# A planned order for the first attention pairs, one index table, two expert halves in a row, and unread matrix products in the tail

## The chip, the cores and the metric

The kernel runs on one core of one Trainium2 chip. The metric is the device time of one execution in microseconds; lower is better. The core's engines work side by side and wait for each other by semaphores: PE (TensorE, matrix products into PSUM), DVE (VectorE), ACT (ScalarE), POOL (GpSimd, which here issues all loads) and SP (SyncE, which issues the stores).

## The reference

Attention over 4 batches of 8 heads, 768 positions of 64 numbers, causal. In some heads ("streaming") a position sees only the first 4 keys and the last 64. Its output, as 3072 rows of 512, goes through a soft mixture of 8 experts with 4 slots each:

```python
scores = np.where(mask, q @ k.T / 8, -1e9)          # mask: causal, or sinks and window
a = softmax(scores);  x = (a @ v)                    # -> x: [3072, 512]
logits = x @ phi                                     # [3072, 32 slots]
d = exp(logits) / column sums;   slot_input = d.T @ x
for e in range(8):
    slot_out[e] = relu(slot_input[e] @ w1[e]) @ w2[e]    # 512 -> 1024 -> 512
out = (exp(logits) / row sums) @ slot_out
```

## The kernel before

**Pairs and quads.** Two heads make a pair (`n`, 16 of them), two pairs a quad (`Q`, 8), four pairs a batch (`b`). For a quad, `load` (L203) brings q, k and v, converting f32 to bf16 on the way; each of the three has two buffers (`raws`), so the load for quad Q + 2 is issued when quad Q has been read (`after_turn`, L560). The first quad is loaded in halves. POOL issues these loads in order, with the expert weights between them (`weights`, L537). The buffers and the mask table lie in the space of the last four w2 matrices, which are therefore loaded last (L571 to L575, L624).

**Steps of a pair.** In the plan's names: `T` turns half a quad of q, k or v with PE transposes (L221), and `e` copies the result from PSUM to SBUF on DVE or ACT (L233). `Tb`/`eb` turn v back into blocks (L244, L252). `Q` makes a unit of 448 score columns for both heads (L268), `x` its exp on ACT (L280), `M` multiplies the four kinds of block by the mask (L286), `V` makes a masked copy of v (L260). `P` is the product with v (L304), `N` divides by the row sum (L315), `X`/`eX` transpose the output (L326, L336). Per batch, `La`, `Lb` and `el` give the logits and their exp, `G`, `D`, `R` the sums over them. `H` builds one head's mask from the tables `delta` and `stream` (`head_mask`, L525, two DVE operations of 256 columns).

**Order.** Nothing is scheduled at run time: class `Plan` (L42) holds the operations of PE, ACT and DVE with costs, dependences, earliest times (`at`) and ranks, and walks through them, always taking the one that can start first. The engines get their work in that order and follow it strictly. PSUM has two slots for scores (`sc`) and two for transposes (`tr`); an operation that takes a slot waits until its former contents are read.

**Before the plan** (L473 to L553): the constants are set, ten products of zeros keep PE busy, q and k of the first half quad are turned, the tables are made on DVE from three index patterns written by POOL, and the masks of heads 0 to 3 are built. The masks of heads 4 to 7 are `H` steps of the plan.

**After the plan** (L624 on): the last batch's dispatch (`slp`), its sums, the slot inputs `siT`; for each half of the experts (`e4`) the product with w1 (`hp`, L665, 32 products of 512 columns), relu on ACT and DVE (`hs`), transposes (`tph`) and their copy `hT`; the product with w2 (`second`, L682) in four calls; the output rows, stored as they come (L704).

Of the kernel before, what the change touches and what calls it, by code (L numbers as in the profile page):

```python
# [38 lines left out]
SWITCH = 0.115  # L39


class Plan:  # L42
# [22 lines left out]
    def build(self):  # L65
        NP, add = self.NP, self.add
        for n in range(NP):
            Q, b, n4 = n // 2, n // 4, n % 4
            for u in range(6):
                if Q:  # L70
                    d = [f"e{t}{Q}.{h}" for t in "qk" for h in range(2)]
                else:
                    d = [f"e{t}0.1" for t in "qk"] if n else []
                add(f"Q{n}.{u}", "PE", 0.19, 0.27, d, n + u / 6, "Q", mode="H", slot=("sc", f"x{n}.{u}"))
                d = [f"Q{n}.{u}"] + ([f"P{n - 2}.1.B"] if u == 0 and n > 1 else [])
                add(f"x{n}.{u}", "ACT", 0.814, 0.95, d, n + u / 6, "x")
            if 2 <= n < 4:
                for a in range(2):
                    add(f"H{n}.{a}", "DVE", 0.8, 0.9, [], n - 1.0, "H")
            hm = [f"H{n}.0", f"H{n}.1"] if 2 <= n < 4 else []  # L80
# [16 lines left out]
        for i, t in enumerate("vqk"):  # L97
            if t == "v":
                self.turn(t, 0, 0, [], 0.0, cost=0.5)
            self.turn(t, 0, 1, [], {"v": 1.0, "q": 0.3, "k": 0.6}[t], cost=0.5)  # L100
        for a in range(2):
            self.turn("b", 0, a, [f"ev0.{a}"], a + 0.5)
        for Q in range(1, NP // 2):
            n = 2 * Q - 1
            for i, (t, h) in enumerate((("q", 0), ("k", 0), ("q", 1), ("k", 1))):
                d = [f"Q{2 * Q - 3}.5"] if Q > 1 else []
                self.turn(t, Q, h, d, n + i / 4, at=(4.0 if t == "q" else 6.0) if Q == 1 else 0.0)
            for h in range(2):
                d = [f"Tb{Q - 1}.1"]
                self.turn("v", Q, h, d, n + 1 + h / 4, at=8.0 if Q == 1 else 0.0)  # L110
            for a in range(2):
                d = [f"P{2 * Q - 3}.1.B", f"V{2 * Q - 3}"] if Q > 1 else []
                self.turn("b", Q, a, [f"ev{Q}.0", f"ev{Q}.1"] + d, n + 1.5 + a / 4)
        for b in range(NP // 4):
# [4 lines left out]
            if b < NP // 4 - 1:  # L119
# [5 lines left out]
                add(f"eR{b}", "DVE", 0.15, 0.25, [f"R{b}"], n + 2.1, "eD")  # L125

    def order(self):
# [44 lines left out]
RANK = {"D": -0.22, "V": 1.15, "x": 2.77, "M": -1.62, "eX": 0.07, "eD": 0.79, "M5": -0.31, "eT": -0.45,  # L172
        "X": 0.66, "P": 0.44, "G": 0.12, "el": -0.31, "L": -0.76, "H": -0.26, "N": -0.18, "eG": 0.8,
        "T": -0.79}
EVAC = {"k1": "ACT"}
# [3 lines left out]
class Attn:  # L179
# [57 lines left out]

    def copy(self, eng, o, i):
        if eng == "ACT":
            self.nc.scalar.copy(o, i)  # L240
        else:
            self.nc.vector.tensor_copy(o, i)  # L242
# [37 lines left out]
    def exp(self, n, u):  # L280
        if u == 0:
            self.pT[n] = self.ptp.tile([128, 2, NPT], BF16, tag="pT", name="pT")
        self.nc.scalar.activation(self.pT[n][:, :, u * UNIT:(u + 1) * UNIT], self.sc.pop((n, u))[:, :, :UNIT],  # L283
                                  ACT.Exp, scale=self.scale)
# [113 lines left out]
def kernel(  # L398
# [75 lines left out]
    nc.sync.dma_start(ri, bass.AP(tensor=ir32, offset=0, ap=[[0, P], [1, 2 * H]]))  # L474
    at.load("q", 0, 0)
    at.load("k", 0, 0)
    with tc.tile_pool(name="setup", bufs=1) as setup:
        iti = setup.tile([P, P], I32, name="iti")
        nc.gpsimd.iota(iti, pattern=[[1, P]], base=0, channel_multiplier=-1)
        at.load("v", 0, 0)  # L480
        at.load("q", 0, 1)
        at.load("k", 0, 1)
        nc.gpsimd.iota(tk[:, 0:1], pattern=[[0, 1]], base=0, channel_multiplier=1)
        tq = setup.tile([P, 256], I32, name="tq")
        nc.gpsimd.iota(tq, pattern=[[128, 2], [1, 16], [16, 8]], base=0, channel_multiplier=0)
        at.load("v", 0, 1)

        zw = msk[:, H - 1, :]
        nc.vector.memset(zw, 0.0)
        zp = at.scp.tile([P, 2, 512], F32, tag="sc", name="zp")  # L490

        def zeros(c):
            for i in range(c):
                nc.tensor.matmul(zp[:, i % 2, :], zw[:, :128], zw, start=True, stop=True)  # L494

        zeros(10)
        nc.vector.memset(quarter, 0.25)
        nc.scalar.activation(colpart[:, 0:1], quarter, ACT.Exp)
        for vb in vbs:
            nc.vector.memset(vb[:, :, :, :, 64:], 1.0)  # L500
        nc.vector.tensor_single_scalar(ident, iti, 0.0, op=ALU.is_equal)
        at.turn("q", 0, 0)
        at.turned("q", 0, 0, "DVE")
        at.turn("k", 0, 0)
        at.turned("k", 0, 0, "ACT")
        zeros(2)

        nc.vector.tensor_single_scalar(tk[:, 1:2], tk[:, 0:1], 7, op=ALU.bitwise_and)
        nc.vector.tensor_single_scalar(tk[:, 2:3], tk[:, 0:1], 3, op=ALU.logical_shift_right)
        nc.vector.tensor_single_scalar(tk[:, 3:4], tk[:, 1:2], 4, op=ALU.logical_shift_left)  # L510
        nc.vector.tensor_tensor(tkf[:, 0:1], tk[:, 2:3], tk[:, 3:4], op=ALU.add)
        nc.vector.tensor_single_scalar(tkf[:, 1:2], tkf[:, 0:1], float(n_sink), op=ALU.is_lt)
        nc.vector.tensor_tensor(tkf[:, 2:3], tkf[:, 0:1], tk[:, 0:1], op=ALU.subtract)
        nc.vector.tensor_scalar(perm, iti, tkf[:, 2:3], None, op0=ALU.is_equal)
        causal = setup.tile([P, 256], BF16, name="causal")
        nc.vector.tensor_scalar(causal, tq, tkf[:, 0:1], 0.0, op0=ALU.subtract, op1=ALU.is_ge)
        nc.vector.tensor_scalar(delta, tq, tkf[:, 0:1], float(window), op0=ALU.subtract, op1=ALU.is_ge)
        nc.vector.tensor_sub(stream, causal, delta)
# [4 lines left out]
    nc.vector.tensor_copy(fmask[:, :, 0], r0)  # L523

# [4 lines left out]

    for t in "qkv":  # L530
        at.load(t, 1)
    for h in (0, 2, 1, 3):
        head_mask(h)
# [8 lines left out]
    phf = at.small.tile([P, 4, ES], F32, tag="phf", bufs=1, name="phf")  # L542
    for hp in range(2):
        for qh in range(2):
            nc.sync.dma_start(phf[64 * hp:64 * hp + 64, 2 * qh:2 * qh + 2, :],
                              moe_phi.rearrange("(qh hp a d) s -> qh hp d a s", qh=2, hp=2, a=2)[qh, hp])
    weights(1)
    nc.gpsimd.tensor_copy(phi, phf)
# [5 lines left out]


# [22 lines left out]
    for name in plan.order():  # L578
# [26 lines left out]
        elif op == "R":  # L605
            at.row_sums(int(arg))
        elif op == "T":
# [3 lines left out]
            else:  # L611
                at.turn(t, Q, h)
                turns[t, Q] = turns.get((t, Q), 0) + 1
                if turns[t, Q] == (1 if Q == 0 and t != "v" else 2):
                    after_turn(t, Q)
        elif arg[0] in "qkvb":
# [20 lines left out]
    at.exp_slots_out(bl)  # L637
    for e4 in range(2):
# [15 lines left out]
    nc.vector.tensor_copy(siT, sip)  # L654
    sctx.close()
# [3 lines left out]
    hTs = []  # L659
    for e4 in range(2):  # L660
# [11 lines left out]
        hv = hs.rearrange("p c f -> p (c f)").rearrange("p (fi fo) -> p fo fi", fo=8)  # L672
        tp = at.trp.tile([P, 8, P], BF16, tag="tr", name="tph")
        for fo in range(8):
            nc.tensor.transpose(tp[:, fo, :], hv[:, fo, :], ident)
# [103 lines left out]
```

## Time and profile before

| | us |
|---|---|
| median of 3 runs | 162.59 (161.79, 167.25, 162.59) |
| the profiled execution | 162.0 |
| its span, first to last instruction | 160.3 |
| busy in the span: PE / DVE / ACT / POOL | 127.5 / 117.1 / 107.4 / 30.6 |
| first exp, last exp (start) | 11.24, about 113.7 |
| first store issued | 140.58 |

Times of single steps are microseconds from the span's start. In a line of the timeline stand the start, the time from first start to last end, the engine, the line, the operation, output and input, how many, and in brackets how long the engine was idle before and what ended that. Matmuls are pipelined, so the shown times of neighbours overlap; the pitch, from one start to the next, is what a queue of them takes. PEclk is the granted clock of PE, 1.00 or 10 tenths being full. DMA moved 26.22 MB of loads by the software queue; its busy share was 0.9 or more in nearly every slice from 4 us to 128 us, and 6.29 MB of output went out after 140.6 us.

The chain of work that ended last is 50% PE, 25% DVE and 16% ACT.

### The profile page before, as it was taken

How to read it: one execution, taken by the hardware profiler on the slowest of the kernel's cores; microseconds unless marked ns; L12 is line 12 of the kernel's file. 1: busy time of each engine (PE TensorE's matmuls, PEld its weight loads, DVE VectorE, ACT ScalarE, POOL GpSimd, SP SyncE). 2: the span in 40 equal slices, each digit the busy share in tenths (PEclk: the TensorE clock that was granted, in tenths of full speed). 3: DMA queues.
4: the chain of work that ended last, by engine and by line, in shares of the span. 5: the costliest groups of instructions: out<-in, count | busy, mean ns of one | idle time of the engine just before them, and what ended most of it. 6: DMA issues, size and time to landing. Idle time of an engine off the chain costs nothing.

```text
span 160.3 us, 5605 instructions
## 1 busy us (share of the span) xinstructions
PE 127.5 (80%) x2506; PEld 87.9 (55%) x2508; DVE 117.1 (73%) x256; ACT 107.4 (67%) x141; POOL 30.6 (19%) x58
## 2 busy tenths in 40 slices
PE   6765999999999998999999998998744866886200
PEld 2344666777777675676777675675532235752000
DVE  1499877999999988999989999978845031267400
ACT  3030779999899988999989998989603014087600
POOL 6941432041050033036200013000510000000000
PEclk9955558999999999999999999999996599999955
DMA  2999999999999999999999999999999960069996
GB/s 35 187 168 213 225 199 230 198 224 208 206 224 203 214 229 197 225 210 204 222 212 220 217 221 211 217 215 217 219 194 196 201 85 0 4 203 342 367 404 255
DMA packets 16087, 32.93 MB, mean 205 GB/s; under 512 B 1728, under 2 KB 8896, under 8 KB 14272
## 3 DMA queue, kind: packets, MB, share of 16 engines
q0 software_dynamic: 11216, 26.22, 86.4%
q1 hardware_dynamic: 4848, 6.37, 11.5%
q8 instruction: 19, 0.31, 0.7%
q14 instruction: 4, 0.03, 0.1%
HBM read 52.50 MB, written 6.29 MB: 367 GB/s over the span
## 4 chain that ended last, share of the span: by engine, by line
PE 50%; DVE 25%; ACT 16%; issue 3%
ACT pT L283 11%; PE sc L276 11%; PE pv L311 9%; DVE pT L302 5%; DVE xb L323 5%; PE tpv L228 3%; PE hp L665 3%; PE tpk L228 3%; PE tpx L332 3%; PE tpq L228 3%; PE zp L494 3%; PE sp L687 3%; DVE w L527 2%; PE tpb L248 2%; ACT ot L731 2%
## 5 line engine op out<-in xcount | busy, mean ns | idle before, releaser
L283 ACT ACTIVATE pT<-sc 128x896 bf16<-128x896 f32 x96 | 81.6, 922 | 9.6 <-PE sc L276 7.8
L276 PE MATMUL sc<-qT,kT 64*128 64x128 bf16 (+4 forms) x352 | 34.2, 281 | 1.1 <-ACT pT L283 0.6
L302 DVE TENSOR_TENSOR pT<-pT,w 128x1024 bf16<-128x1024 bf16 (+1 forms) x64 | 32.1, 519 | 3.3 <-ACT pT L283 2.7
L311 PEld LDWEIGHTS <-pT 128*128 128x128 bf16 x672 | 25.1, 97 | 10.1 <-issue 7.8
L311 PE MATMUL pv<-vb,pT 128*128 128x65 bf16 x352 | 28.7, 193 | 1.2 <-DVE xb L323 1.1
L228 PEld LDWEIGHTS <-w 96*64 96x64 bf16 (+1 forms) x864 | 22.7, 121 | 9.4 <-issue 5.9
L311 PE MATMUL pv<-vf,pT 128*128 128x65 bf16 x320 | 24.4, 194 | 0.3 <-issue 0.3
L276 PEld LDWEIGHTS <-kT 64*128 64x128 bf16 x352 | 12.3, 96 | 8.4 <-issue 1.4
L323 DVE TENSOR_TENSOR xb<-pv,rs 128x768 bf16<-128x768 f32 x16 | 15.3, 957 | 0.6
L240 ACT COPY kT<-tpk 128x768 bf16<-128x768 bf16 x9 | 7.2, 799 | 9.6 <-PE tpk L228 9.6
L208 POOL DMA_DIRECT2D w<-in_q_dram x7 | 4.6, 657 | 35.8 <-PE sc L276 31.9
L263 DVE TENSOR_TENSOR vf<-vb,fmask 128x528 bf16<-128x528 bf16 x16 | 11.2, 699 | 0.0
L242 DVE COPY qT<-tpq 128x768 bf16<-128x768 bf16 x16 | 8.8, 551 | 3.2 <-PE tpq L228 3.1
L248 PE MATMUL tpb<-ident,vT 128*128 128x128 bf16 x96 | 8.7, 231 | 2.8 <-DVE vT L242 2.8
L228 PE MATMUL tpk<-ident,w 96*64 96x96 bf16 (+1 forms) x288 | 9.9, 216 | 1.2 <-DMA w<-in_k_dram 0.9
L228 PE MATMUL tpv<-ident,w 96*64 96x96 bf16 (+1 forms) x288 | 9.4, 219 | 1.4 <-issue 1.3
L228 PE MATMUL tpq<-ident,w 96*64 96x96 bf16 (+1 forms) x288 | 9.8, 216 | 0.4 <-DMA w<-in_q_dram 0.4
L332 PE MATMUL tpx<-ident,xb 128*128 128x128 bf16 x96 | 8.1, 220 | 2.3 <-DVE xb L323 2.3
L242 DVE COPY vb<-tpb 128x768 bf16<-128x768 bf16 x16 | 8.9, 553 | 1.1 <-PE tpb L248 0.8
L242 DVE COPY vT<-tpv 128x768 bf16<-128x768 bf16 x16 | 8.4, 552 | 1.5 <-PE tpv L228 1.4
L337 DVE COPY xT<-tpx 128x768 bf16<-128x768 bf16 x16 | 8.8, 552 | 0.6 <-PE tpx L332 0.6
L248 PEld LDWEIGHTS <-vT 128*128 128x128 bf16 x96 | 5.9, 102 | 4.9 <-DVE vT L242 3.3
(87 smaller groups left out, 139.7 us busy)
## 6 DMA issues: line engine op xcount, KB each, us to landing
w<-in_moe_w_dram POOLq DMA_DIRECT2D x14, 1024.0 KB, 18.0
out_dram<-ot SPq DMA_DIRECT2D x12, 256.0 KB, 3.1
out_dram<-ot SPq DMA_DIRECT2D x6, 512.0 KB, 4.9
w<-in_q_dram POOLq DMA_DIRECT2D x7, 384.0 KB, 11.3
w<-in_k_dram POOLq DMA_DIRECT2D x7, 384.0 KB, 10.5
w<-in_v_dram POOLq DMA_DIRECT2D x7, 384.0 KB, 15.3
w<-in_moe_w_dram POOLq DMA_DIRECT2D x4, 512.0 KB, 16.2
w<-in_q_dram POOLq DMA_DIRECT2D x2, 192.0 KB, 5.1
```

The source lines that it names most:

```text
L228: self.nc.tensor.transpose(tp[64 * hp:64 * hp + 64, x, :], raw[p0:p0 + rows, hp, s * 64:s * 64 + 64], self.ident[p0:p0 + rows, p0:p0 + rows])
L240: self.nc.scalar.copy(o, i)
L242: self.nc.vector.tensor_copy(o, i)
L248: self.nc.tensor.transpose(tp[:, i].rearrange("p h d -> p (h d)"), vT[:, 6 * a + i, :], self.ident)
L263: self.nc.vector.tensor_mul(vf, self.vbs[n // 2 % 2][:, n % 2, :, :4, :], fm.to_broadcast([128, 2, 4, VW]))
L276: nc.tensor.matmul(sc[:, hh, o:o + w], kT[ps, (g0 + j) * 128:(g0 + j + 1) * 128], qT[ps, g0 * 128 + q0:g0 * 128 + q0 + w], start=True, sto ...
L283: self.nc.scalar.activation(self.pT[n][:, :, u * UNIT:(u + 1) * UNIT], self.sc.pop((n, u))[:, :, :UNIT], ACT.Exp, scale=self.scale)
L302: nc.vector.tensor_mul(v, v, m)
L311: self.nc.tensor.matmul(pv[:, hh, i * 65:(i + 1) * 65], pT[:, hh, o:o + 128], (vb if i - j <= 1 else vf)[:, j, :65], start=(j == 0), stop= ...
L323: nc.vector.tensor_mul(x, pv[:, :, :, :64], rs.to_broadcast([128, 2, 6, 64]))
L332: self.nc.tensor.transpose(tp[:, i * 128:(i + 1) * 128], self.xb[b][:, i, n4 * 128:(n4 + 1) * 128], self.ident)
L337: self.nc.vector.tensor_copy(self.xT[n // 4][:, n % 4], self.tp.pop(("x", n, 0)))
```

## The change

- **First pairs.** The turns of the first half quad (`q0.0`, `k0.0`), which stood ahead of the plan, become steps of it, and so do the masks of heads 0 to 3. The plan gets a list `FIRST` of times from which the first nine turns may start, and 5.2 for the masks. `k0.0` is copied half by DVE, half by ACT (`first_k`). `Q` of pair 0 waits for both k0.0 and its own copy. The loads of quad 1 are issued earlier in the program text.
- **Ranks.** `RANK` has new numbers, and `EVAC` sends the copy of each quad's first back turn (`b0`) to ACT.
- **Tables.** One index pattern, `iti` (column minus row), serves for `ident`, `perm`, the row numbers, and `delta` and `stream`; the patterns `tk` and `tq` and the table `causal` go. `delta` is made in two halves of 128 columns; the second half of what was `causal` is a constant 1.
- **phi** is loaded by POOL's queue with conversion, in four loads; before, SP loaded it in f32 and POOL converted it.
- **Tail.** The two halves' products with w1 follow each other, and then come both halves' transposes. Products that nothing reads (`Z` in the plan: 5, 2 and 3; `fill(2)` twice after it) multiply `perm` with 512 columns of w1. Two of the zero products at the start go.

```diff
+FIRST = (5.4, 7.0, 8.2, 9.2, 10.1, 11.0, 13.0, 15.0, 17.0)
...
-                    d = [f"e{t}0.1" for t in "qk"] if n else []
+                    d = [f"e{t}0.{n}" for t in "qk"]
...
-                d = [f"Q{n}.{u}"] + ([f"P{n - 2}.1.B"] if u == 0 and n > 1 else [])
+                d = [f"Q{n}.{u}"] + ([f"P{n - 2}.1.B"] if n > 1 else [])
...
-            if 2 <= n < 4:
+            if n < 4:
                 for a in range(2):
-                    add(f"H{n}.{a}", "DVE", 0.8, 0.9, [], n - 1.0, "H")
+                    add(f"H{n}.{a}", "DVE", 0.8, 0.9, [], n - 1.0, "H", at=5.2)
...
+        for i, (t, a, r) in enumerate((("q", 0, -9.0), ("k", 0, -9.0), ("v", 0, 0.0),
+                                       ("q", 1, 0.3), ("k", 1, 0.6), ("v", 1, 1.0))):
+            self.turn(t, 0, a, [], r, cost=0.5, at=FIRST[i])
...
+        n = NP - 1
+        for i, (after, c) in enumerate(((f"P{n}.1.B", 5), (f"X{n}", 2), (f"Lb{n // 4}", 3))):
+            add(f"Z{i}.{c}", "PE", 0.22 * c, 0.2, [after], n + 9.0, "Z", slot=("sc", f"Z{i}.{c}"))
...
-EVAC = {"k1": "ACT"}
+EVAC = {"k1": "ACT", "b0": "ACT"}
...
+    def first_k(self):
+
+        dst = self.blocked("k", 0).rearrange("c g (s p) -> c s g p", p=8)[:, :, :6]
+        tp = self.tp.pop(("k", 0, 0)).rearrange("c s (g p) -> c s g p", p=8)
+        self.nc.vector.tensor_copy(dst[:, :8], tp[:, :8])
+        self.nc.scalar.copy(dst[:, 8:], tp[:, 8:])
...
-        nc.gpsimd.iota(tk[:, 0:1], pattern=[[0, 1]], base=0, channel_multiplier=1)
-        tq = setup.tile([P, 256], I32, name="tq")
-        nc.gpsimd.iota(tq, pattern=[[128, 2], [1, 16], [16, 8]], base=0, channel_multiplier=0)
...
-        zeros(2)
...
-        nc.vector.tensor_scalar(causal, tq, tkf[:, 0:1], 0.0, op0=ALU.subtract, op1=ALU.is_ge)
-        nc.vector.tensor_scalar(delta, tq, tkf[:, 0:1], float(window), op0=ALU.subtract, op1=ALU.is_ge)
-        nc.vector.tensor_sub(stream, causal, delta)
...
+    nc.vector.tensor_single_scalar(tk[:, 0:1], iti[:, 0:1], -1, op=ALU.mult)
...
+    rel = iti.rearrange("m (p s) -> m s p", s=16)
+    for c, d in ((0, 0), (1, 128)):
+        nc.vector.tensor_scalar(delta[:, 128 * c:128 * c + 128].rearrange("m (s p) -> m s p", p=8), rel,
+                                tkf[:, 2:3], float(window - d), op0=ALU.subtract, op1=ALU.is_ge)
+    nc.vector.tensor_scalar(stream[:, :128].rearrange("m (s p) -> m s p", p=8), rel, tkf[:, 2:3], 0.0,
+                            op0=ALU.subtract, op1=ALU.is_ge)
+    nc.vector.tensor_sub(stream, stream, delta)
...
-    for h in (0, 2, 1, 3):
-        head_mask(h)
...
-            nc.sync.dma_start(phf[64 * hp:64 * hp + 64, 2 * qh:2 * qh + 2, :],
-                              moe_phi.rearrange("(qh hp a d) s -> qh hp d a s", qh=2, hp=2, a=2)[qh, hp])
-    weights(1)
-    nc.gpsimd.tensor_copy(phi, phf)
+            nc.gpsimd.dma_start(phi[64 * hp:64 * hp + 64, 2 * qh:2 * qh + 2, :],
+                                moe_phi.rearrange("(qh hp a d) s -> qh hp d a s", qh=2, hp=2, a=2)[qh, hp])
...
+    def fill(c):
+
+        fp = at.scp.tile([P, 2, 512], F32, tag="sc", name="fp")
+        for i in range(c):
+            nc.tensor.matmul(fp[:, i % 2, :], perm, w1s[0][:, 0, :512], start=True, stop=True)
...
     at.exp_slots_out(bl)
+    fill(2)
...
     nc.vector.tensor_copy(siT, sip)
+    fill(2)
...
-        hv = hs.rearrange("p c f -> p (c f)").rearrange("p (fi fo) -> p fo fi", fo=8)
+        hvs.append(hs.rearrange("p c f -> p (c f)").rearrange("p (fi fo) -> p fo fi", fo=8))
+    for e4 in range(2):
         tp = at.trp.tile([P, 8, P], BF16, tag="tr", name="tph")
         for fo in range(8):
-            nc.tensor.transpose(tp[:, fo, :], hv[:, fo, :], ident)
+            nc.tensor.transpose(tp[:, fo, :], hvs[e4][:, fo, :], ident)
```

In the order of the built program the first steps on each engine are: on DVE, the tables, H0.0, H0.1, q0.0's copy, H1.0, half of k0.0's copy, H1.1, v0.0's copy, H2.0, q0.1's copy, H2.1, H3.0, v0.1's copy, and then the first mask product; on PE, Tq0.0, Tk0.0, Tv0.0, Q0.0, Q0.1, Tq0.1, Tb0.0, Q0.2, Q0.3, Tk0.1, Tv0.1, Q0.4, Tq1.0, Tb0.1, Q0.5, Q1.0, Tk1.0, Q1.1, Tq1.1, Tk1.1, Q1.2, Q1.3, Tv1.0, Tv1.1 and the first `P`; on ACT, half of k0.0's copy, two exps, b0.0's copy, an exp, k0.1's copy, five exps, k1.1's copy.

## The prediction

> **What bounds the kernel now.** I read the slices of the page first, then the timeline of the first 30 us, then busy time by stage, then the timeline of the tail.
>
> ```profile
> PE   6765999999999998999999998998744866886200
> DVE  1499877999999988999989999978845031267400
> ACT  3030779999899988999989998989603014087600
> PEclk9955558999999999999999999999996599999955
> DMA  2999999999999999999999999999999960069996
> ```
>
> A digit is 4 us. From slice 8 to 28 PE, DVE and ACT are all nearly full: a balanced stage. Idle time is in the head (slices 1 to 5) and in the tail (29 to 38), and there the clock row falls to 5. The head, in the timeline:
>
> ```profile
> 9.41 4.08 DVE L527 SCALAR_TENSOR_TENSOR w<-delta,r,stream 128x256 bf16<-128x256 bf16 x10
> ...
> 11.24 0.92 ACT L283 ACTIVATE pT<-sc 128x896 bf16<-128x896 f32 x1 [2.72 <-PE sc L276]
> ...
> 14.02 0.82 PE L248 MATMUL tpb<-ident,vT 128*128 128x128 bf16 x6 [2.83 <-DVE vT L242]
> ...
> 16.56 1.73 ACT L283 ACTIVATE pT<-sc 128x896 bf16<-128x896 f32 x2
> ```
>
> Ten mask operations hold DVE for 4.1 us while vT waits to leave PSUM, so PE stands idle 2.8 us, and ACT has one exp at 11.24 and the next at 16.56. Then the stages:
>
> ```profile
> 29.30:113.70 84.40, 79.59 (x1752) 57.73 (x1748) 78.96 (x162) 79.06 (x98) 14.89 (x25) 1.00 1.06 214
> 118.00:124.50 6.50, 3.13 (x50) 1.97 (x53) 3.16 (x16) 1.72 (x3) 0.00 (x0) 0.74 1.34 195
> 124.40:128.10 3.70, 3.60 (x32) 1.08 (x32) 0.02 (x1) 0.00 (x0) 0.00 (x0) 0.52 1.47 202
> ```
>
> After the length the columns are PE, PEld, DVE, ACT, POOL, granted clock, DMA share, GB/s. From pair 2's first exp to pair 15's last ACT is 94% busy (79.06 of 84.40). The experts' first product runs at clock 0.52:
>
> ```profile
> 124.48 3.60 PE L665 MATMUL hp<-w,siT 128*32 128x512 bf16 x32 [1.72 <-DVE siT L654]
> ...
> 128.14 0.69 ACT L669 ACTIVATE hs<-hp,emask 128x512 bf16<-128x512 f32 x1 [4.84 <-PE hp L665]
> 128.86 0.75 DVE L670 TENSOR_SCALAR hs<-hp,emask 128x512 bf16<-128x512 f32 x1 [4.43 <-ACT hs L669]
> 129.66 0.70 PE L675 MATMUL tph<-ident,hs 128*128 128x128 bf16 x8 [1.58 <-DVE hs L670]
> 130.30 1.91 PE L665 MATMUL hp<-w,siT 128*32 128x512 bf16 x32
> ```
>
> The same 32 products take 3.60 us there and 1.91 at 130.30, at full clock. From the first store (140.6) on, output DMA sets the pace (331 GB/s to the end), so what is won before it is won at the end.
>
> **Part 1: the head.** After `ident` (ends 3.25) DVE now makes the tables from `iti`. Before, 14 operations (L508 to L523) took 6.60 to 9.41, 2.81 us. Now 16, two of them halves of delta: I take 3.0 us, to 6.25. Then the planned order: two H, q0.0's copy, an H, half of k0.0's copy. An H is two mask operations of 4.08/10 = 0.41, so 0.82; a copy's pitch is 0.47. q0.0 leaves at 6.25 + 1.63 = 7.9 (before: 6.12), H1.0 from 8.35, the half copy from 9.15. No row shows half a copy: between 0.24 and 0.55, taken 0.3. The ACT half waits in the built program for DVE, so the halves run one after the other: another 0.4 to 0.8, taken 0.5. kT is there at 10.0, first exp at 10.6 (before 11.24); but Q0.1 follows at once, so the second exp comes at 11.4 instead of 16.56.
>
> From there PE is the limit, if its clock is 0.5 as before. Its order up to the first pv product has 10 score units of 0.49 (4.9), three 48-row turns of 0.98 (2.9), two backs of 0.75 (1.5), four 96-row turns of 0.78 (3.1), v's two (1.42): 13.9 us from 10.0, so 23.9. Before: 25.56. That is 1.65 us. Had the clock come back sooner, ACT is next: up to pair 2's first exp it has 12 exps of 0.82 and four copies of 0.71, 12.6 us from 10.6, and 2.2 us of waits for PE and DVE that I find by following the order row by row: 25.4 against 29.32, or 3.9 us. The gain lies between 1.65 and 3.9; I take 2.7, since the old head spent 4 us of idle PE inside the windows from which the clock is judged and the new one has none after 10.0. The two zero products dropped after k0.0's turn (0.38 us) fed nothing, and the clock fell at 8.5 with them. Below nothing: each further 3.4 us at half clock costs half of that PE work, 1.7 us.
>
> POOL: two iotas (0.19 and 0.60) go, so v0.1's load is issued 0.56 us sooner. Four phi loads of about 0.65 each come in, with the cast (0.29) gone; each waits for an earlier load, the last for v0.1. Queued behind are sum4, used at 122, and q2, k2, w1_1, v2. DMA share is above 1.0 from 4 us on, so those loads only join a queue: at about 205 GB/s, v2, after 5.6 MB, lands near 31 either way, and its turn was at 35.3 and will be near 32.6. That cover is thin; without it each microsecond late is one lost. SP loses its four phi issues, which ended at 3.9: nothing waits.
>
> **Part 2: the steady stage.** The first back copy of each quad moves from DVE to ACT. Between 29.3 and 113.7 that is six: DVE loses 6 x 0.47 = 2.8 us, ACT gains 6 x 0.71 = 4.3 (pitch of the k copies there, a copy of the same size). ACT's 79.06 becomes 83.3 of 84.4. If its 5.3 us of idle all go, the stage takes 83.3: 1.1 less. If they stay, 88.7: 4.3 more. Most idle before exps is for score products (7.8 of 9.6 us in all, partly in the head), which wait on a PE that DVE's lighter load helps; so nearer the first: +1.0.
>
> **Part 3: the tail.** The unread products lie in gaps: 5 of them (512 columns, about 0.21 each by the opf pairs' 0.22 steps) after 116.75, while N15 runs on DVE to 118.01; 2 while eX15 copies; 3 while `el` is on ACT; 2 and 2 around `sip`. The last two need the PSUM slot that ACT reads until 123.2, and siT is only ready at 124.4. Cost nothing; at half clock the first five would take 2.1 us and hold X15 up by 0.9. What they should bring is clock: full at 118, it fell at 121.1, and came back at 128.0.
>
> The Trainium skill, TensorE: Matmul & The Clock Gate, Part 1 ("The HAM clock gate"), says that the clock falls after an idle window of about 3.4 us. No PE gap here before 121.1 is longer than 1.5 us, so the trace disagrees with plain idleness. By the rule the fall would not be curable by filling such gaps and the tail would give 2.4 us; by the row it is a matter of how much is done.
>
> I take the row: PE was busy 3.13 of 6.50 us at 118 to 124.5, mostly with small products, and 114 to 118, with 2.2 of 4.0 us busy and two gaps of about 1 us, kept its clock. The filling adds 14 x 0.21 = 3.0 us, 2.1 of them before 121.
>
> With it: slp 0.2 sooner (DVE's eight reductions then hold the rest), hp at 124.2, first half to 126.1, second straight behind to 128.0. hs of the second half takes 0.69 + 0.75 with the hand-over, to 129.5; its transposes and the first half's hT copy, now queued behind that hs on DVE, end at 130.2. The products of w2 start at 130.25; before, 134.45. So 4.2 us: 1.7 clock, 2.2 that the second half no longer waits for the first half's relu and transposes (6.3 us from hp's end to w2 became 4.15), 0.25 slp. If the clock falls anyway, hp ends at 128.0, the second at 129.9, w2 starts at 132.1: 2.35.
>
> What is late next: the last w2 halves. They land near 127 and 132.6 (issued at 113.3 and 115.9, 13.9 and 16.8 us to landing), and are used at 138.1 and 141.28. With 5.9 us won the second is 2.8 us clear; the gain is capped at 8.7.
>
> **Sum.** The profiled execution's own time is 162.0 (span 160.3 and 1.7 around it), 0.6 below the median 162.59. 162.0 - 2.7 + 1.0 - 4.2 = 156.1.
>
> **Rivals.**
> - *The clock falls all the same in the tail.* For it: it fell with no long gap. Against: 14 wide products. 162.0 - 2.7 + 1.0 - 2.35 = 157.9. Chance 0.17.
> - *ACT becomes the bound.* For it: 98.7% needed at the old pace. Against: its waits are for engines that get lighter. 156.1 + 3.3 = 159.4. Chance 0.15.
> - *The head's clock comes back early.* 156.1 - 1.2, and the stage without ACT idle, 2.1 less: 152.8, which the w2 landing (153.3) stops. Chance 0.11.
> - *Slower: the half clock lasts into the pairs.* Place: the windows after 22 us, where turns and small pv products, not wide score products, fill PE. Price 1.7 us for each 3.4 us. Four windows eat the gain; from six on it is slower by over 2%: 156.1 + 10.2 = 166.3. For it: one of the three times is 167.25, so some such thing happens. Against: the clock rose at 25.5, as pv began, and never fell in the stage. Chance 0.06.
>
> The Trainium skill, TensorE: Matmul & The Clock Gate, Part 4 ("PE-mode transpose"), says that transposes do not count as PE work for the gate; here PE is 100% busy from 16 to 25, much of it transposes, at clock 0.50, which agrees. By it no turn in the new head would help the clock.
>
> Forecast 0.51, at 154.6 to 157.6. About 2%, 3.3 us, is what a measurement of this kernel can tell from no change: below 158.7 is faster. Faster: 0.51 + 0.11 + most of the first rival (0.12) = 0.74; slower 0.06; the rest, 0.20, same. The range that leaves out 0.1 at each end is 153.6 to 160.0.
>
> **What would show it.** Masks L535 spread between copies from 6.2 on; the second exp near 11.4; PE busy without a gap from 10 to 25; pair 2's first exp near 26.6; ACT at 97% or more in the stage and last exp near 112; clock 1.0 from there through L678's 64 products, both halves near 1.9 us; second-layer products 4.2 us nearer to the last exp. Wrong if the clock row is 5 beyond slice 6 or the exps wait for v2.

## The result and the profile after

The changed kernel takes 157.05 us (median of 155.6, 156.91, 157.18 and 157.25) against 164.63 (161.79, 162.59, 166.68 and 167.25). Two of the four runs before, 166.68 and 167.25, were in a slower state of the chip and are left out of the ratio, which is 0.966, with a 95% interval of 0.956 to 0.977: faster. Its profiled execution took 157.25 (span 155.5), where the one before took 162.0 (span 160.3), so the span lost 4.8 us; the forecast was 5.9.

The slices of the page of the changed kernel, 3.9 us to a digit:

```profile
PE   6869999969999897999999989998978688885300
DVE  3995999965998898899698899888873623467300
ACT  3038799967999998999999989999932232287500
PEclk9975599987999999999999999999999999999855
DMA  2999999999999999999999999999999996089995
```

The half clock of the head now ends in slice 5, and the tail keeps its clock until PE is nearly done (slice 37). New is a dent in slices 8 and 9: PE falls off in slice 8, DVE, ACT and the clock in both. The head, in the timeline of the changed kernel:

```profile
7.85 0.54 DVE L253 COPY qT<-tpq 128x768 bf16<-128x768 bf16 x1
...
9.11 0.34 DVE L246 COPY kT<-tpk 128x384 bf16<-128x384 bf16 x1
...
9.48 0.48 ACT L247 COPY kT<-tpk 128x384 bf16<-128x384 bf16 x1 [7.19 <-DVE kT L246]
...
10.61 1.73 ACT L294 ACTIVATE pT<-sc 128x896 bf16<-128x896 f32 x2 [0.65 <-PE sc L287]
```

Two exps follow each other at 10.61. The last ten exps of the attention, before and after, end at 114.73 and 114.00:

```profile
106.52 8.21 ACT L283 ACTIVATE pT<-sc 128x896 bf16<-128x896 f32 x10
...
105.67 8.33 ACT L294 ACTIVATE pT<-sc 128x896 bf16<-128x896 f32 x10
```

Busy time by stage (length, PE, PEld, DVE, ACT, POOL, clock, DMA share, GB/s), from pair 2's first exp to pair 15's last, then two stretches of the tail:

```profile
25.20:113.10 87.90, 81.43 (x1754) 58.23 (x1752) 76.32 (x155) 82.91 (x106) 15.74 (x27) 0.98 1.06 214
118.00:123.60 5.60, 3.92 (x49) 1.70 (x47) 3.06 (x15) 1.71 (x3) 0.00 (x0) 1.00 1.32 194
123.60:127.30 3.70, 3.69 (x66) 1.75 (x67) 0.75 (x1) 0.69 (x2) 0.00 (x0) 1.00 1.46 198
```

The difference adds up from these rows and the earlier one (29.3 to 113.7): pair 2 starts 4.1 sooner, the stage from there on is 87.9 long instead of 84.4 and gives 3.5 back, and from pair 15's last exp to the end of the span it is 42.4 instead of 46.6, 4.2 less. 4.1 - 3.5 + 4.2 = 4.8. The start of the second layer before, and then the tail of the changed kernel:

```profile
134.43 1.94 PE L687 MATMUL sp<-w,hT 128*32 128x256 bf16 x64
```

```profile
123.61 3.64 PE L678 MATMUL hp<-w,siT 128*32 128x512 bf16 x64 [1.29 <-DVE siT L666]
...
127.30 0.69 ACT L682 ACTIVATE hs<-hp,emask 128x512 bf16<-128x512 f32 x1 [1.04 <-PE hp L678]
...
128.83 0.71 PE L689 MATMUL tph<-ident,hs 128*128 128x128 bf16 x8 [0.93 <-DVE hs L683]
129.46 1.94 PE L701 MATMUL sp<-w,hT 128*32 128x256 bf16 x64
```

All 64 products of the first layer take 3.64 us, where 32 alone took 3.60 before. And the dent of slice 8, PE's and ACT's rows:

```profile
32.99 0.87 PE L232 MATMUL tpv<-ident,w 96*64 96x96 bf16 x32 [1.55 <-DMA w<-in_v_dram]
...
34.39 0.92 ACT L294 ACTIVATE pT<-sc 128x896 bf16<-128x896 f32 x1 [1.33 <-PE sc L287]
...
36.18 0.92 ACT L294 ACTIVATE pT<-sc 128x896 bf16<-128x896 f32 x1 [0.88 <-PE sc L287]
```

PE waits 1.55 us for the values of quad 2, and from 33.8 to 37.1 its clock is 0.5.

### The profile page after: what moved, and what is told of

Read it like the earlier page. It is cut to its first block, busy times and chain, and to the rows that moved or that the text cites. A ratio compares the mean times of both kernels' runs of the same rounds, so it can differ in the third digit from the quotient of the medians.

```text
span 155.5 us, 5623 instructions
## 1 busy us (share of the span) xinstructions
PE 128.5 (83%) x2520; PEld 87.9 (57%) x2520; DVE 113.7 (73%) x252; ACT 111.7 (72%) x149; POOL 32.3 (21%) x59
## 4 chain that ended last, share of the span: by engine, by line
PE 44%; ACT 17%; DMA 16%; DVE 9%; issue 4%; POOL 4%; POOLq 0%; ACTq 0%
ACT pT L294 12%; PE pv L322 11%; PE sc L287 10%; DMA w<-in_moe_w_dram 10%; DMA w<-in_v_dram 7%; PE tpx L343 3%; PE tpb L259 3%; PE sp L701 3%; PE hp L678 2%; POOL w L215 2%; DVE xb L334 2%; PE tpv L232 2%; PE lg L356 2%; ACT ot L745 2%; DVE pT L313 2%
## 5 line engine op out<-in xcount | busy, mean ns | idle before, releaser
L294 ACT ACTIVATE pT<-sc 128x896 bf16<-128x896 f32 x96 | 82.9, 927 | 6.6 <-PE sc L287 5.9
L313 DVE TENSOR_TENSOR pT<-pT,w 128x1024 bf16<-128x1024 bf16 (+1 forms) x64 | 32.6, 519 | 6.7 <-ACT pT L294 6.3
L287 PE MATMUL sc<-qT,kT 64*128 64x128 bf16 (+4 forms) x352 | 34.8, 283 | 2.5 <-ACT kT L247 0.9
L322 PEld LDWEIGHTS <-pT 128*128 128x128 bf16 x672 | 25.2, 98 | 8.7 <-issue 8.0
L322 PE MATMUL pv<-vb,pT 128*128 128x65 bf16 x352 | 29.2, 195 | 0.3 <-issue 0.2
L232 PEld LDWEIGHTS <-w 96*64 96x64 bf16 (+1 forms) x864 | 21.9, 119 | 11.5 <-issue 7.3
L322 PE MATMUL pv<-vf,pT 128*128 128x65 bf16 x320 | 25.0, 196 | 0.0
L232 PE MATMUL tpv<-ident,w 96*64 96x96 bf16 (+1 forms) x288 | 8.3, 207 | 3.3 <-DMA w<-in_v_dram 1.6
L733 ACT ACTIVATE ot<-oph,rrow 128x256 f32<-128x256 f32 x12 | 4.6, 482 | 5.2 <-PE oph L727 5.2
L343 PEld LDWEIGHTS <-xb 128*128 128x128 bf16 x96 | 6.1, 100 | 2.8 <-DVE xb L334 2.5
L470 POOL DMA_DIRECT2D w<-in_moe_w_dram x6 | 3.2, 536 | 20.1 <-PE tpq L232 15.7
```

The source lines that it names most:

```text
L232: self.nc.tensor.transpose(tp[64 * hp:64 * hp + 64, x, :], raw[p0:p0 + rows, hp, s * 64:s * 64 + 64], self.ident[p0:p0 + rows, p0:p0 + rows])
L287: nc.tensor.matmul(sc[:, hh, o:o + w], kT[ps, (g0 + j) * 128:(g0 + j + 1) * 128], qT[ps, g0 * 128 + q0:g0 * 128 + q0 + w], start=True, sto ...
L313: nc.vector.tensor_mul(v, v, m)
L322: self.nc.tensor.matmul(pv[:, hh, i * 65:(i + 1) * 65], pT[:, hh, o:o + 128], (vb if i - j <= 1 else vf)[:, j, :65], start=(j == 0), stop= ...
L343: self.nc.tensor.transpose(tp[:, i * 128:(i + 1) * 128], self.xb[b][:, i, n4 * 128:(n4 + 1) * 128], self.ident)
```

## The experiments

Each starts from the changed kernel unless it says otherwise. "Stage" below is the stretch of the first row above, from pair 2's first exp to pair 15's last.

The kernels were measured in three groups: phi_sp, no_fill, seq_halves and b0_dve; phi_late, phi_late_b0, before_tail and masks_first; the four whose names begin with w. Each group has its own runs of the kernel before (medians 162.6, 165.51 and 164.34), and the ratios are against these. The changed kernel itself ran only beside the 164.63 above. So a time of a group does not compare directly with 157.05. By the ratios a distance from the changed kernel's 0.966 is known to about 2 us; times within a group compare better. Each trace is of one execution, which can differ from the other three of its kernel.

### Does the tail bring what was forecast?

**no_fill** takes the 14 unread products out (the planned `Z` and both `fill(2)`).

```diff
-        for i, (after, c) in enumerate(((f"P{n}.1.B", 5), (f"X{n}", 2), (f"Lb{n // 4}", 3))):
-            add(f"Z{i}.{c}", "PE", 0.22 * c, 0.2, [after], n + 9.0, "Z", slot=("sc", f"Z{i}.{c}"))
...
-    fill(2)
```

> All 14 unread products of the tail are left out. Theory (they hold the clock): the granted clock falls to 0.5 between 117 and 125 us, the 64 products with w1 take 5.4 us instead of 3.64, the time is 1.7 to 2.0 us longer: 158.9 us. Rival (the clock holds by chance of the window, or by the shorter gaps alone): hp still takes 3.6 us, 157.0 us.

159.62 us, ratio 0.978 (0.967 to 0.990): by the ratios 1.2% above the changed kernel, some 2 us. Two windows of 3.41 us of no_fill, the window of the changed kernel at the same time, and the timeline of no_fill:

```profile
115.76:119.17 3.41, 1.77 (x36) 1.18 (x36) 0.66 (x2) 0.81 (x1) 0.00 (x0) 1.00 1.05 199
119.17:122.58 3.41, 1.59 (x20) 0.92 (x22) 2.59 (x14) 0.90 (x2) 0.00 (x0) 0.50 1.35 191
```

```profile
115.68:119.09 3.41, 3.02 (x50) 1.83 (x47) 1.75 (x3) 0.00 (x0) 0.35 (x1) 1.00 1.07 208
```

```profile
122.16 5.51 PE L672 MATMUL hp<-w,siT 128*32 128x512 bf16 x64 [1.72 <-DVE siT L661]
```

Without the products PE is busy 1.77 of 3.41 us and its clock falls at 119.17; with them it is busy 3.02 and the clock stays. The 64 products then take 5.51 instead of 3.64. From the end of the last exp (112.55) to the second layer (129.89) it is 17.34 us in no_fill and 15.46 in the changed kernel: 1.9 for the clock.

**seq_halves** puts each half's transposes directly behind its own products again.

```diff
         hvs.append(hs.rearrange("p c f -> p (c f)").rearrange("p (fi fo) -> p fo fi", fo=8))
-    for e4 in range(2):
         tp = at.trp.tile([P, 8, P], BF16, tag="tr", name="tph")
```

> Each half's transposes follow its own product again, the unread products stay. Theory (the second half waited for the first half's relu and transposes): first w2 product about 2.2 us later after the start of hp, 159.2 us. Rival (w2's loads or the hand-over of hs set the start of the w2 products): 157.2 us.

159.31, ratio 0.978 (0.968 to 0.988): again 1.2% above, some 2 us. Its timeline:

```profile
121.39 1.91 PE L678 MATMUL hp<-w,siT 128*32 128x512 bf16 x32 [1.28 <-DVE siT L666]
...
124.88 0.71 PE L688 MATMUL tph<-ident,hs 128*128 128x128 bf16 x8 [1.58 <-DVE hs L683]
125.52 1.91 PE L678 MATMUL hp<-w,siT 128*32 128x512 bf16 x32
...
129.01 0.72 PE L688 MATMUL tph<-ident,hs 128*128 128x128 bf16 x8 [1.58 <-DVE hs L683]
129.66 1.94 PE L700 MATMUL sp<-w,hT 128*32 128x256 bf16 x64
```

From the first product to the second layer it is 8.27 us, against 5.85 side by side: PE waits for the relu twice. From the end of the last exp (111.77) to the second layer it is 17.89, 2.4 more than in the changed kernel.

**before_tail** is the kernel before with nothing but the new tail (the same `Z`, `fill` and loop).

> The kernel before with only the tail changed: unread products and the two expert halves in a row. Theory (the tail's gain stands by itself): 4.2 us faster than before, with hp's 64 products near 3.6 us at full clock; about 158.4 us where before gives 162.6. Rival (the w2 loads, which end near 132 us, hold the tail, or the fill does not hold the clock with the old order): 1 to 2.5 us faster.

159.97, ratio 0.969 (0.954 to 0.984). In its timeline

```profile
126.62 3.64 PE L679 MATMUL hp<-w,siT 128*32 128x512 bf16 x64 [1.29 <-DVE siT L667]
...
132.49 1.94 PE L702 MATMUL sp<-w,hT 128*32 128x256 bf16 x64
```

the 64 products are at full clock. The tail alone is thus worth 3.1% of some 164 us, about 5 us with an interval of 2.6 to 7.6. In the trace, from the end of the last exp (117.04) to the second layer, it is 15.45 us, as in the changed kernel (15.46), and 4.2 less than before (its exps ended 2.3 late in that execution, so its own span lost only 1.9). The tail is the larger part of the gain and does not depend on the new head.

### Does the spreading of the masks bring the head?

**masks_first** makes the masks of heads 0 to 3 in one row ahead of the plan, as before, with all else changed.

```diff
-            if n < 4:
+            if 2 <= n < 4:
...
+    for h in (0, 2, 1, 3):
+        head_mask(h)
```

> The masks of heads 0 to 3 are built in one row ahead of the plan again; tables, arrival times and tail as in the changed kernel. Theory (the head's gain comes from the copies no longer waiting behind masks): DVE's first copy at 9.5 instead of 7.85, first exp near 11.4, pair 2's first exp 0.8 to 1.5 us later, 158 us. Rival (the earlier tables alone bring it): 157.0 us.

161.39, ratio 0.981 (0.970 to 0.992): 1.5% above the changed kernel, some 2.4 us. In its group before_tail, with the same tail and the old head, has 159.97. The loss in the head is far more than expected. Its timeline:

```profile
6.24 4.83 DVE L535 SCALAR_TENSOR_TENSOR w<-delta,r,stream 128x256 bf16<-128x256 bf16 x12
...
13.76 0.92 ACT L294 ACTIVATE pT<-sc 128x896 bf16<-128x896 f32 x1 [0.65 <-PE sc L287]
```

DVE keeps the copies out until 11, the first exp comes 3.15 later, and the half clock then lasts until 29.55: pair 2 starts near 31.4 instead of 25.2. So in the new order the masks must be spread: in one row they cost 6.2 us there, and half of it is still there at the last exp (116.99 against 114.00). How much of the gain over the old head the spreading brought is not shown, since masks_first is a worse head than the old one. It has twelve mask operations ahead of all copies. The kernel before had copied q0.0 and k0.0 before its masks (from 6.12 and 7.72), and its first exp came at 11.24, not at 13.76.

### What takes the stage's 3.5 us?

**phi_sp** loads phi through SP's queue in float32 and casts on POOL, as before.

```diff
-            nc.gpsimd.dma_start(phi[64 * hp:64 * hp + 64, 2 * qh:2 * qh + 2, :],
+            nc.sync.dma_start(phf[64 * hp:64 * hp + 64, 2 * qh:2 * qh + 2, :],
...
+    nc.gpsimd.tensor_copy(phi, phf)
```

> phi is loaded by SP in f32 and converted by POOL again, all else as in the changed kernel. Theory (late load): the four phi loads put v of quad 2 behind the landing of the first expert weight (issue at 22.83, landing 32.95, PE waits 1.55 us and its clock falls for 3.4 us). Without them v is issued before 19 us, PE does not wait near 33 us, the clock stays 1.00 from 20 us on, the stretch from pair 2's first exp to the last exp gets 2 to 3 us shorter: 154.6 us. Rival (ACT is the limit): the stage is long because ACT has six more copies, the wait is caught up later: 156.6 us or more.

156.15, ratio 0.963 (0.955 to 0.970): between the two that were expected. Timeline and stage of phi_sp:

```profile
11.10 1.05 PE L232 MATMUL tpv<-ident,w 48*64 48x48 bf16 x32 [3.34 <-DMA w<-in_v_dram]
```

```profile
28.80:113.40 84.60, 80.36 (x1754) 57.83 (x1752) 76.16 (x156) 82.49 (x106) 15.04 (x25) 1.00 1.07 214
```

In this execution the very first values came late, and pair 2 started at 28.8. Yet its last exps end 0.3 us after those of the changed kernel, since the stage is 84.6 long. Neither theory had this: in this execution a start 3.6 us later is made up all but whole.

**b0_dve** puts the first back copy of each quad on DVE again (`EVAC` without `b0`), which also moves the planned order.

> The first back copy of each quad stays on DVE (EVAC as before the change; the plan's order follows). ACT loses eight copies of 0.71 us, DVE gains eight of 0.47. Theory (the three engines are balanced, the late load is what costs): between 156.3 and 158.0 us. Rival (ACT is the limit of the stage): pair 2's first exp to the last exp about 3 us shorter, 154 us.

157.95, ratio 0.964 (0.950 to 0.977), from 155.75 to 160.3: it settles nothing.

**phi_late** queues phi's four loads on POOL behind the values of quad 2, so that nothing of phi stands ahead of them.

```diff
             if t == "v":
                 at.load("v", Q + 2)
+                if Q == 0:
+                    load_phi()
```

> The four phi loads stay on POOL but come after the load of v for quad 2. Theory (their place in the queue makes v late): first exp near 10.6 as in the changed kernel, v of quad 2 issued before 19 us, no wait of PE for it near 33 us; 2.5 to 3 us off the stage and nothing lost in the head: 154.3 us. Rival (ACT's added copies make the stage long, or the load simply arrives late): 156.5 us or more.

155.71, ratio 0.946 (0.936 to 0.957). POOL's and PE's timeline of phi_late (its profiled execution took 157.75, two above its other three):

```profile
15.98 0.65 POOL L212 DMA_DIRECT2D w<-in_v_dram  x1
...
33.28 0.87 PE L232 MATMUL tpv<-ident,w 96*64 96x96 bf16 x32 [1.85 <-DMA w<-in_v_dram]
```

In the changed kernel the same load is issued at 22.83. Issued 6.9 us sooner it is no sooner there. So in this execution the place of the load on POOL did not make it late, and the 5.6 MB up to its last byte are what is left; w_late below takes 1 MB of them away. What the three faster executions did left no trace.

**phi_late_b0** adds `EVAC` without `b0` to that.

> As phi_late, and the first back copy of each quad on DVE again. Theory (with the load on time ACT is the engine that limits the stage): 1 to 2 us faster than phi_late, 153 us. Rival (balance: DVE pays what ACT saves): as phi_late or up to 1.5 us slower.

156.56, ratio 0.948 (0.933 to 0.963): no gain over phi_late. With the copy on DVE the planner also puts other steps ahead, and ACT's timeline shows a stop that the changed kernel does not have (the profiled execution took 158.33, about two above the median):

```profile
29.62 3.56 ACT L294 ACTIVATE pT<-sc 128x896 bf16<-128x896 f32 x4 [4.36 <-PE pv L322]
```

Pair 2 thus starts at 29.6, and the stage is 84.5 long, like those of other late starts (table below). Giving ACT less work brought no time; what it would do to a stage that starts at 25 is not shown.

**w_early** and **w_late** move one expert weight, 1 MB, ahead of quad 2's loads or behind them; the total is the same.

```diff
-    weights(1)
+    weights(2)
     for hp in range(2):
```

```diff
-    weights(1)
     for hp in range(2):
```

> The changed kernel with the opposite edit: two expert weights (2 MB) instead of one are queued ahead of quad 2's loads, the total is the same. Theory (bytes ahead bind, each microsecond late is one lost): v of quad 2 lands near 38 instead of 33, PE waits about 6.5 us there instead of 1.55, ACT idles with it, and the time is 160.5 to 163, 3.5 to 6 above the changed kernel. Rival (the place matters little, since the later work catches up or the loads are reordered): within 1.5 of the changed kernel, 155.5 to 158.5.

161.14, ratio 0.983 (0.975 to 0.991): 1.7% above the changed kernel, some 2.7 us. PE's timeline of w_early:

```profile
29.61 0.85 PE L232 MATMUL tpq<-ident,w 96*64 96x96 bf16 x16 [4.45 <-DMA w<-in_q_dram]
```

It is the queries of quad 2 that come late first, by 4.45 us, and the last exps end at 118.55, 4.55 after those of the changed kernel. Against w_late, of the same group, the time is 3.9 longer.

> The changed kernel with one edit: the first expert weight (1 MB) is not queued ahead of quad 2's loads; the counter of weight loads makes it up at the end, so the same 12 are loaded, each one place later. Theory (the bytes ahead of v of quad 2 bind, not where its load is issued: issued at 22.83 in the changed kernel and at 15.98 with phi late, its data was waited for until 32.99 and 33.28 all the same): 1 MB less at about 210 GB/s lands it near 28, so the 1.55 us that PE waits at 33, the 2.07 us that ACT then idles (0.92, 0.88, 0.27) and the half clock of 33.8 to 37.1 are gone, the last exps end near 111.5 instead of 114.0, and the time is 154.0 to 155.5 against 157.05. Rival (ACT is full through the stage and takes up what the stall leaves): the wait goes, the last exps end at 113.3 or later, and the time is 156.3 to 157.3. Second rival (the DMA queue is short of work with 1 MB less in it): the last weights land later than 132, and the time is 157.5 or more.

157.22, ratio 0.961 (0.954 to 0.967), not told apart from the changed kernel's 0.966 (0.956 to 0.977): the time of the first rival. But its mechanism is not the rival's. PE's timeline and the stage of w_late:

```profile
34.63 0.22 PE L322 MATMUL pv<-vb,pT 128*128 128x65 bf16 x2 [0.86 <-issue]
...
47.84 0.37 PE L287 MATMUL sc<-qT,kT 64*128 64x256 bf16 x4 [1.53 <-issue]
```

```profile
25.20:112.80 87.60, 80.14 (x1754) 57.88 (x1752) 76.06 (x155) 82.71 (x106) 15.56 (x26) 1.00 1.06 210
```

The values are not waited for and the clock never falls, yet the stage is 87.6. ACT still stands idle 4.9 of it: PE has new waits, 4.6 us between 25 and 112, which the profile puts down to nothing ("issue"); in the changed kernel these are 2.1.

**w_late_phi_late** has both edits.

> The edit of w_late, and phi's four loads queued after v of quad 2 as in phi_late. Theory (bytes ahead decide, the place of four loads of 8 KB does not): the same as w_late to 0.8 us, 153.8 to 155.5, no PE wait near 33. Rival (phi's loads on POOL cost by themselves, by the landings that they and what follows them on POOL wait for): over 1 us below w_late, with v of quad 2 issued several us sooner.

156.91, ratio 0.957 (0.949 to 0.964), as w_late to 0.3.

**w_last** asks whether all this comes from the busy DMA engines: it takes the expert weights out of the larger part of the stage, by dropping `weights(...)` ahead of the plan and from all but the last turns.

```diff
-    weights(1)
...
-                weights(NWQ[Q] - 1)
...
-                weights(1)
```

> The changed kernel with the loads of the expert weights taken out of the attention stage: the first 12 MB are queued only after the last keys and queries are turned (about 93 us), nothing is left out. The experts must then wait for them: 16.8 MB at about 210 GB/s are 80 us, so the time itself will be 175 to 200 and is not compared; what is read is the stage. Theory (what arrives through the busy DMA engines sets the stage: v of quad 2, and in w_late the waits of PE for nothing that the profile shows, 4.6 us between 25 and 112 against 2.1 in the changed kernel): v of quad 2 is not waited for, those waits sum to 0.7 or less, ACT waits for score products 2.5 us or less (4.3 and 4.2 in the changed kernel and w_late), no window at half clock after 25, and the last exps end at 110.5 to 112.2 instead of 114.0 and 113.7. Rival (the engines' own work and hand-overs set it, and any lead of the head is lost again): PE's unexplained waits stay at 1.5 or more, ACT waits 3.5 or more, the last exps end at 113 to 114.2.

175.7 us (one execution), and the weights are queued from 69.4, sooner than I had written: the DMA share is 0.5 to 0.8 from 25 to 65, and over 1.0 again from 75 on. The stage of w_last, and ACT's waits between 25 and 114 (us in total, times, longest):

```profile
25.70:109.40 83.70, 79.61 (x1754) 57.60 (x1752) 75.98 (x156) 81.97 (x106) 15.02 (x26) 1.00 0.82 157
```

```profile
ACT pT L294 <- PE sc L287: 1.3, 4, 0.7
```

With the same work on every engine the stage is 83.7 instead of 87.9, the last exps end at 110.3 instead of 114.0, and ACT is busy 98% of it. The waits for score products fall from 4.3 to 1.3. The waits put down to nothing are 1.2 in sum, not the 0.7 expected, but all of them come when the weights are back in the queue:

```profile
87.32 0.33 PE L232 MATMUL tpk<-ident,w 96*64 96x96 bf16 x7 [0.59 <-issue]
93.79 0.54 PE L232 MATMUL tpv<-ident,w 96*64 96x96 bf16 x17 [0.57 <-issue]
```

Between 25 and 69 w_last has none, and PE does not wait for data; the changed kernel has both there, w_late only the unexplained waits. Where the time goes is seen in the start of the n-th of the 96 exps:

| kernel | 13th | 19th | 25th | 37th | 49th | 73rd | 96th |
|---|---|---|---|---|---|---|---|
| changed | 25.31 | 31.34 | 39.67 | 51.69 | 65.04 | 90.21 | 113.05 |
| w_late | 25.30 | 31.18 | 37.68 | 51.24 | 64.23 | 89.95 | 112.73 |
| seq_halves | 25.63 | 31.50 | 38.09 | 50.16 | 63.15 | 88.05 | 110.83 |
| w_last | 25.89 | 31.77 | 37.29 | 49.33 | 61.75 | 86.32 | 109.38 |

From the 13th exp to the last the changed kernel loses 4.25 us to w_last. 2.8 of it goes between the 19th and the 25th, where PE waits for the values and then runs at half clock, and 0.9 between the 37th and the 49th, where PE stops for 0.73 at 60.50 for nothing that the profile names. In w_late the losses follow the stops one by one: 1.0 behind the 0.86 at 34.63, 1.5 behind the 1.53 at 47.84. So the stage was held by data that came late, by the half clock behind that, and by stops that were absent in the one execution without the traffic.

The stages side by side, from the same two marks (within 0.3 us of the exact starts):

| kernel | pair 2's first exp | pair 15's last | length | ACT busy |
|---|---|---|---|---|
| before | 29.3 | 113.7 | 84.4 | 79.06 |
| before_tail | 30.6 | 116.1 | 85.5 | 79.38 |
| b0_dve | 32.0 | 116.1 | 84.1 | 78.51 |
| phi_late_b0 | 29.6 | 114.1 | 84.5 | 78.42 |
| masks_first | 31.4 | 116.1 | 84.7 | 82.33 |
| phi_sp | 28.8 | 113.4 | 84.6 | 82.49 |
| seq_halves | 25.6 | 110.9 | 85.3 | 82.50 |
| no_fill | 25.3 | 111.6 | 86.3 | 82.49 |
| w_late_phi_late | 25.8 | 112.8 | 87.0 | 82.54 |
| changed | 25.2 | 113.1 | 87.9 | 82.91 |
| w_late | 25.2 | 112.8 | 87.6 | 82.71 |
| phi_late | 25.2 | 113.6 | 88.4 | 82.91 |
| w_early | 25.2 | 117.6 | 92.4 | 82.67 |
| w_last | 25.7 | 109.4 | 83.7 | 81.97 |

Started at 28.8 or later, the stage takes 84.1 to 85.5 and has no stop for data. Started at 25 to 26 with the weights in the queue it takes 85.3 to 88.4, and 92.4 in w_early; with the weights held back until 69 it takes 83.7. seq_halves, whose program in this stretch is the changed kernel's, waited 1.12 us for the same values and its clock did not fall. Its pv products, and those of the changed kernel behind the wait:

```profile
33.83 0.27 PE L322 MATMUL pv<-vb,pT 128*128 128x65 bf16 x3
...
34.28 0.35 PE L322 MATMUL pv<-vb,pT 128*128 128x65 bf16 x3
```

Its 25th exp starts 1.6 us sooner than the changed kernel's, though its 19th started 0.2 later. So the fall of the clock and the 0.43 us of longer wait are together worth some 1.7 us, and the fall comes in one execution and not in another.

The best version of all runs is phi_late, 155.71 against the changed kernel's 157.05. They never ran beside each other, and their intervals (0.936 to 0.957 and 0.956 to 0.977) touch: that it is faster than the changed kernel is likely and not shown; that it is faster than the kernel before is shown.

## Why the prediction was right, point by point

The time, 157.05, is 0.95 above the 156.1 forecast and inside the forecast's own 154.6 to 157.6. The tail was right in size and mechanism. The head gave 1.4 us more than its term and the stage took 2.5 us more than its term. That these two errors partly cancel, and the sum with the measured sizes is 162.0 - 4.1 + 3.5 - 4.2 = 157.2, is luck in part: with the head's term as forecast, the stage alone would have put the time at 158.6, out of the range.

- **Tables and first copies.** Forecast 7.9, 9.15 and 10.6 for q0.0's copy, the half copy and the first exp; measured 7.85, 9.11 and 10.61. This part came from counting operations.
- **The head's clock.** 2.7 taken between 1.65 and 3.9; measured 4.1, just beyond the upper bound. The half clock ended at 20.11, not with the first pv product, which came at 21.97 instead of 23.9. The chosen value leaned to PE at half clock all the way; the ACT chain (25.4) was the one that held. The rival of the early clock had the mechanism, without its gain in the stage.
- **POOL and the values of quad 2.** The prediction had a landing near 31 and a turn near 32.6 and called the cover thin. The data let PE go at 32.99, after a wait of 1.55: two microseconds later than estimated. "Without it each microsecond late is one lost" holds for more lateness (w_early: 4.45 us late, last exps 4.55 later), not for less: without the 1.55 (w_late) the last exps end only 0.3 sooner, since the next stops took their place. That phi's loads "only join a queue" fits the trace of phi_late, which moved them: the values came no sooner.
- **The stage, the step that was mis-sized: +1.0 taken, +3.5 measured.** ACT's work came out as forecast (83.3 against 82.9). The other half failed: that ACT's idle time would mostly go, because PE, for which it waits, is helped by a lighter DVE. 5.0 of the 5.3 us stayed. DVE did get lighter, 76.3 instead of 79.0, but PE did not wait for DVE: it waited for data, for its clock, and, most of all in w_late, for what the profile does not name. The prediction had warned of the data and given it no price in the sum. In w_last, with the weights held back until 69, the stage is 0.7 shorter than before, near the first bound (1.1 less).
- **The tail.** 4.2 forecast. From the end of pair 15's last exp (114.73 before, 114.00 after) to the second layer's first product (134.43, 129.46) it was 19.70 us and is 15.46: 4.24. Taking the parts out again makes the same stretch 1.9 (clock) and 2.4 (side by side) longer in the traces, where 1.7 and 2.2 were forecast; in the times each costs about 2. The Trainium skill, TensorE: Matmul & The Clock Gate, Part 1, speaks of an idle window; in no_fill no PE gap in the five microseconds before the fall is longer than 1.32 us, and the filling cures it, so the row that the prediction followed was the right one.
- **What is late next.** The last w2 halves were not waited for; the first store is issued at 135.6 instead of 140.6.
- **The rivals.** "ACT becomes the bound" is true of the stage only when little else stops it (98% in w_last, 97.5% in phi_sp); in the changed kernel ACT is at 94%, no fuller than before, not at the 97% that the prediction named as a sign, and its last exp starts at 113.1, not near 112. The slower rival's mechanism, half clock while pv products fill PE, is seen in the profiled execution of phi_late_b0, where the half clock lasts until 28.36 and ACT stands 4.36 us once; in the changed kernel it lasts one window, after 33.8.
- **The sign given for being wrong** ("the clock row is 5 beyond slice 6 or the exps wait for v2") did come, both of it, and at the step that was off: the half clock lasts from 33.76 to 37.17, which the row shows as 8 and 7 because it straddles two slices, and the exps wait behind v2. By that sign the path of the prediction was wrong at this step, though the time was right.

Left open: what PE's waits for nothing are, what exactly makes the clock fall (the section on the hardware has the rows), and whether the kernel before loses some of its own 5.3 us of idle ACT to the same traffic.

## What to carry to other kernels

A head start is worth only as much as the data that is there for it: when the DMA engines are full from end to end, set the turn of every early load against its landing before counting the gain. Where one wait is taken away and the time stays, look for the next one in the same stretch; a run without the traffic tells quickly whether engines or arrivals set the pace. And PE's clock in a tail of small steps was held here with unread products, in gaps that existed anyway.

## What the runs showed of the hardware

- The half clock begins and ends on a grid of 3.41 us (before: 8.49, 25.56, 121.13, 127.96). Windows on this grid: the changed kernel ahead of its fall at 33.76, seq_halves around its wait of 1.12, and of the kernel before the one ahead of the fall at 121.13, one in the middle of its tail, and the one ahead of the fall at 8.49:

```profile
30.35:33.76 3.41, 1.86 (x57) 1.36 (x51) 2.04 (x5) 2.71 (x4) 1.18 (x2) 1.00 1.10 207
31.02:34.43 3.41, 2.29 (x61) 1.67 (x58) 2.50 (x6) 2.70 (x4) 1.65 (x3) 1.00 1.12 210
117.72:121.13 3.41, 1.57 (x36) 1.18 (x36) 0.85 (x2) 0.81 (x1) 0.00 (x0) 1.00 1.18 188
127.96:131.37 3.41, 1.83 (x32) 1.12 (x32) 1.44 (x2) 0.69 (x1) 0.00 (x0) 1.00 0.84 114
5.08:8.49 3.41, 2.26 (x79) 1.48 (x80) 2.23 (x11) 0.77 (x1) 3.14 (x6) 1.00 1.23 182
```

  PE busy 1.57, 1.77 (no_fill) and 1.86 us was followed by a fall, 2.29 was not: the shorter wait of seq_halves fell into a window with more work. But 1.83 of products with w1 kept the clock, and 2.26 of zero products and small turns did not. So the busy time of a window alone does not decide; what else does is not shown.
- The clock row can miss a stretch. In seq_halves it shows full clock through the whole head, but its turns of 96 rows take 0.85 us for 16 transposes up to 20.1 and 0.53 from 25.5 on, as in the changed kernel, whose row shows half clock there. The durations decide.
- PE stops at the same place in the program, whenever it gets there: in front of the same score products, at 60.50 in the changed kernel (0.73), 59.69 in w_late (0.38), 61.10 in phi_sp (0.38) and 65.39 in w_early (0.99). In each of these kernels the queue of instructions moves 19 packets with 0.31 MB in all, so 16 KB each; between 74 and 93 us of seq_halves one comes about every 6 us. The Trainium skill, Runtime: NRT & Kernel Launch, "Instruction fetch mechanics", names blocks of that size and calls their fetching mostly hidden. That these stops are a block that comes late through the same busy engines fits w_last, where there are none while the queue holds no weights; no run shows it directly.
